# Attention and two mixers on one core: first weight blocks of the second mixer on another queue, token rows and operand steps in another order

## The chip, the cores and the metric

The kernel runs on one core of a Trainium2 chip. The metric is device time in microseconds (us). A run is one execution; the number given for a kernel is the median of its runs. One further execution was taken with the hardware profiler, and all rows come from that one.

## The reference

Three stages follow each other, for 2 batches of 768 tokens:

- clustered attention, 8 heads of 64: queries and keys get the best of 16 centroids; scores between different clusters are masked; softmax; product with `v`;
- a first mixer on the 512 channels: `u = x + (xT U V)T`, then `u + relu(u w_ch1) w_ch2` with 2048 hidden channels;
- a second mixer: `u = x + (relu(xT w_tok1) w_tok2)T` over tokens with 256 hidden rows, then `u + relu(u w_ch1) w_ch2` with 1536 hidden channels.

The change touches the passage from the channel part of the first mixer to the second mixer, and the channel part of the second mixer.

## The kernel before

Every large product is made of three matmuls on TensorE: a value is split into a rounded part ("hi") and the rest ("lo"), and hi x hi, hi x lo and lo x hi are added in PSUM. ScalarE rounds (`rnd(act, ...)`, L80), VectorE or GpSimd subtracts for the rest (`sub`, L87). A pair of these is called a cut: `cut(i, x, eng)` (L1030) returns the two steps, the second on `eng`.

**First mixer, channel part.** The order is a generator, `half_slots` (L888): 96 half-slots (`END`, L983), each either `hidden(k)` or `outmm(k)` of one of 48 units of 128 hidden channels, 12 matmuls of 512 columns each. The third pass (units 32 to 47) streams its weights from a scratch tensor in DRAM, `scr_a`: `feed` (L792) issues one load of 512 KB on ScalarE's DMA queue after most half-slots, into three slots used in turn. The counter `done` is the number of half-slots emitted. The last three are `hidden(47)` (done = 93), `outmm(46)` (94) and `outmm(47)` (95); after the last, four VectorE adds (L838) complete batch 1 of the residual `x2`.

**Beside it.** SyncE's queue (SP) stores the prepared second-mixer weights to `scr_b`: each `quad` (L616) converts a block and stores it in three transfers, 256, 512 and 1024 KB (L650 to L652). From half-slot 66 on, the token part of batch 0, `tok(0)` (L904), and the steps of `build_u(0)` (L1024) run beside the half-slots. `build_u(b)` makes the seven left operands of a seven-product (Strassen-like) scheme for the second mixer's channel part, `ops_u[b]`, from the four quarters `B` of `x2[b]`: three cuts of sums and quarters in a queue `todo` of 18 steps, popped one or two per half-slot; the last four (the cuts of operands 3 and 4) are left for the loop after the half-slots.

**Passage.** At done = 93, `turn_over` (L1048) opens the buffers of the second mixer and `load1(0)` to `load1(4)` are issued on SP's queue: `load1(n)` (L1069) fetches the n-th block of first-layer weights into one of five buffers `w1b` (four in a tile called `ring`, one in `wx`). Blocks 0, 1, 2 and 4 have 512 KB, block 3 has 256 KB. Later blocks are issued by `h_mm` on SP's queue as a buffer comes free. The program gives all transfers of both queues eight completion counters in turn, so a transfer can be issued only when the one eight before it has landed.

Then a loop of 14 steps (L1220) does the first-layer products of the first two pairs: `h_mm` (L1092), six matmuls of 384 columns into one PSUM bank, and `h_out` (L1108), which combines the seven products on ScalarE and VectorE. Beside them run the last four steps of `todo` (i = 1 and 2) and `tok(1)`, two of its steps at i = 1 to 8. The first six steps of `tok(1)` are its token rows: four transposes of `x2[1]` into PSUM bank 6 or 7 in turn, a copy on ScalarE (L916), a subtraction on VectorE (L917) that frees the bank.

**Second mixer, channel part.** Six runs `(b, k)` (L1236), three per batch, 14 steps each. A step does `h_mm` and `h_out` of the run after (`nxt`) and `o_mm` and `o_out` of this run. `o_out` (L1183) is a VectorE add of a PSUM bank into `x2`. `o_mm` of step i writes a bank that `o_out` of an earlier step must have read: four steps earlier inside a run, but two steps earlier at a run's start (the last products, steps 12 and 13, use the same banks as the first of the next run). During the runs 0 and 1 the 18 steps of `build_u(1)` are popped after `o_out`: one each at steps 5 to 13 of run 0, two each at steps 8 to 12 of run 1. Run 2 is the first to use them, in its `h_mm`. In `h_out`, s = 5 and s = 6 (steps 5, 7, 12 and 13) end with VectorE steps that only later products need.

All instructions of an engine run in the order written; a DMA issue stands in its engine's order too.

Of the kernel before, what the change touches and what calls it, by code (L numbers as in the profile page):

```python
# [16 lines left out]
ALU = mybir.AluOpType  # L17
# [9 lines left out]
def tile_cluster_attention__then__two_mixers(  # L27
# [996 lines left out]
    def build_u(b):  # L1024

        B = {(i, j): x2[b][:, 2 * i : 2 * i + 2, ts(j, HS)] for i in range(2) for j in range(2)}
        o = {i: ops_u[b][pos(i)] for i in ORDER}
        t = [fz[:, 768 * i : 768 * i + 768].rearrange("p (c n) -> p c n", c=2) for i in range(2)]

        def cut(i, x, eng):  # L1030
            hi, lo = o[i][:, 0], o[i][:, 1]
            return [lambda: rnd(act, hi, x), lambda: sub(eng, lo, x, f32(hi))]

        def add(o, x, y, op):
            return [lambda: dve.tensor_tensor(out=o, in0=x, in1=y, op=op)]  # L1035

        early, last = cut(4, t[1], dve), []
        if b == 0:
            early, last = last, early
        return (cut(1, B[0, 0], pool) + cut(2, B[1, 0], pool) + add(t[0], B[0, 0], B[0, 1], ALU.subtract)  # L1040
                + add(t[1], B[1, 1], t[0], ALU.add) + cut(6, t[1], dve) + add(t[1], B[1, 0], t[1], ALU.subtract) + early
                + cut(5, t[0], dve) + add(t[0], B[1, 1], B[0, 1], ALU.subtract) + cut(7, t[0], pool) + cut(3, B[1, 1], pool) + last)

    gfree = [x.rearrange("p (h n) -> p h n", h=2) for x in (qk_[:, ts(i, 2 * HS)] for i in range(14))]
    gs, behind = {}, []
# [20 lines left out]
    seq2 = [(b, k, c) for b, k in runs for c in range(4)]  # L1066
    at1, at2 = {}, {}

    def load1(n):  # L1069
        if n < len(seq1):  # L1070
            b, pr, c = seq1[n]
            ch = HCHUNKS[c]
            m, s0 = len(ch), min(STORED.index(i) for i in ch)
            x = w1b[n % len(w1b)][:, 0 : 512 * m]
            sp.dma_start(f32(x), scr2[pr, 0, :, 512 * s0 : 512 * (s0 + m)])
            for i in ch:
                at1[b, pr, i] = x[:, ts(STORED.index(i) - s0, 512)].rearrange("p (h n) -> p h n", h=2), n, i == ch[-1]

# [29 lines left out]
    def h_out(b, pr, s):  # L1108
# [28 lines left out]
        elif s == 2:  # L1137
            held_[0] = tmp()
            act.copy(held_[0], x)
        elif s == 3:  # L1140
            held_[3] = tmp()
            act.copy(held_[3], x)
        elif s == 4:
            new(3)
            dve.tensor_tensor(out=held_[3], in0=x, in1=held_[3], op=ALU.add)
            act.activation(held_[3], held_[3], AF.Relu)
            rnd(act, hi(3), held_[3])
            sub(dve, lo(3), held_[3], f32(hi(3)))
        elif s == 5:
            new(5, 6)  # L1150
            held_[5], held_[6] = tmp(), tmp()
            dve.tensor_tensor(out=held_[0], in0=x, in1=held_[0], op=ALU.add)
            relu_less(held_[5], held_[0], held_[1], ALU.subtract)
            rnd(act, hi(5), held_[5])
            sub(dve, held_[6], held_[3], held_[5])
            sub(dve, lo(5), held_[5], f32(hi(5)))
            cut(6, held_[6])
        else:
            new(2, 4, 7)
            top(2, x)  # L1160
            low(2, x)
            relu_less(held_[1], x, held_[6], ALU.subtract)
            relu_less(held_[5], held_[0], held_[3], ALU.subtract)
            behind.extend([lambda h=held_[5], c=cut: c(7, h), lambda h=held_[1], c=cut: c(4, h)])

    def o_mm(b, k, s, j):
        w, n, ends = at2[b, k, ORDER[s]]
# [35 lines left out]
    while done < END:  # L1203
        next(bg[1], None)
        next(t, None)
        if done == END - 3:
            for x in bg:
                for _ in x:
                    pass
            turn_over()  # L1210
            for n in range(len(w1b)):
                load1(n)
        k = done - first_tok
        for _ in range(int(16 <= k < 20) + 2 * int(k >= 20)):
            if len(todo) > 4:
                todo.pop(0)()
        advance(done + 1)

    t = tok(1)
    for i in range(14):  # L1220
        pr, s = divmod(i, 7)
        h_mm(0, pr, s)
        h_out(0, pr, s)
        for _ in range(2 * (0 < i < 3)):
            todo.pop(0)()
        for _ in range(1 + (1 <= i < 9) if i else 0):
            next(t, None)
        if i == 9:
            load2(0)
# [2 lines left out]
        pass  # L1232
    for n in range(2, len(w2b)):
        load2(n)
    todo = []
    for r, (b, k) in enumerate(runs):  # L1236
        nxt = runs[r + 1] if r + 1 < len(runs) else None
        if (b, k) == (0, 0):
            todo = build_u(1)
        for i in range(14):  # L1240
            if nxt:
                pr, s = divmod(i, 7)
# [1 line left out]
                h_mm(nxt[0], pr, s)  # L1244
            s_, j = divmod(i, 2)
            o_mm(b, k, s_, j)
            if nxt:
                for x in {6: (), 7: (6, 7)}.get(i, (i,)):
                    h_out(nxt[0], 2 * nxt[1] + x // 7, x % 7)
            if not nxt:  # L1250
                flush()
            o_out(b, k, s_, j)
            send(2 if nxt else 0)
            for _ in range(int(r == 0 and 4 < i) + 2 * int(r == 1 and i > 7)):
                if todo and (r == 1 or len(todo) > 9):
                    todo.pop(0)()
    send(0)


# [39 lines left out]
```

## Time and profile before

| what | value |
|---|---|
| runs | 742.27, 741.26, 742.25 us; median 742.25 us |
| profiled execution | 742.89 us, of which its span (first to last instruction) is 741.1 us |
| TensorE busy | 724.3 us, 98% of the span |
| VectorE, ScalarE, GpSimd busy | 72%, 55%, 27% |
| moved by DMA | 165.36 MB, mean 223 GB/s |
| chain that ended last | 84% TensorE, 8% VectorE, 3% DMA, 3% ScalarE |

TensorE is nearly always busy, so what the kernel can lose or win without other arithmetic lies in the short stretches in which TensorE stands. In a timeline row the two numbers ahead are the start and the length in us; `x12` is the number of instructions merged into the row; the bracket at the end is the idle time of the engine before the row and what ended it. `PE` is TensorE, `DVE` VectorE, `ACT` ScalarE, `POOL` GpSimd; `ACTq` and `SPq` are the DMA issues of ScalarE's and SyncE's queues. Rounding and subtraction have one line each for the whole program (L80 and L87), so they are told apart by what they write. In the passage `u`, `wx`, `qk`, `vz` are places of operands of `build_u(0)`, `ug` those of the token rows, `mid` and `fz` temporaries, `xn` the residual.

### The profile page before, as it was taken

Reading aid. Unit: us, or ns where it says so; the run is one execution under the profiler, and the core shown is the slowest. Engines: PE = TensorE matmul, PEld = TensorE weight load, DVE = VectorE, ACT = ScalarE, POOL = GpSimd, SP = SyncE. Lnnn points to the kernel's source line nnn. Section 1 sums busy time; section 2 is a strip of 40 time slices with the busy share of each in tenths; the row PEclk is TensorE's granted clock in tenths of the full one; section 3 lists DMA queues with packets and bytes.
Section 4 is the critical chain, followed back from the end, with each engine's and each line's share of the span. In section 5 each row is a group of like instructions: output and inputs, shape, how many; then the busy total and the mean of one; then the engine's idle time right before and its main releaser. Section 6 shows DMA issues by size and latency. Waiting matters only on the chain.

```text
span 741.1 us, 11133 instructions
## 1 busy us (share of the span) xinstructions
PE 724.3 (98%) x4046; PEld 601.7 (81%) x4046; DVE 534.0 (72%) x814; ACT 404.4 (55%) x699; POOL 201.7 (27%) x169
## 2 busy tenths in 40 slices
PE   8999999999999999999999999999999989999997
PEld 6666766776777788888888888888779989899997
DVE  7868988877886458769679586698365677765564
ACT  6678778867788455454555363543253435344330
POOL 6232252322211122423222312223012412221121
PEclk9999999999999999999999999999999999999999
DMA  6898588785303353967684989799726877697745
GB/s 175 197 196 225 147 206 206 222 217 124 76 14 119 117 212 120 376 227 284 236 319 172 331 324 374 251 364 386 287 91 217 302 250 236 200 300 270 264 128 164
DMA packets 55862, 165.36 MB, mean 223 GB/s; under 512 B 7648, under 2 KB 16736, under 8 KB 52224
## 3 DMA queue, kind: packets, MB, share of 16 engines
q1 hardware_dynamic: 50768, 147.05, 61.6%
q10 hardware_dynamic: 5040, 17.60, 6.3%
q8 instruction: 32, 0.52, 0.3%
q14 instruction: 22, 0.18, 0.1%
HBM read 103.61 MB, written 41.94 MB: 196 GB/s over the span
## 4 chain that ended last, share of the span: by engine, by line
PE 84%; DVE 8%; DMA 3%; ACT 3%; issue 1%; POOL 0%; SPq 0%; DVEq 0%; ACTq 0%; POOLq 0%
PE ps L75 74%; PE ps L350 8%; DVE qk L87 1%; DMA qk<-scr_a 1%; DMA qk<-pt 1%; DVE xn L1187 1%; ACT qk L80 1%; DVE fz L1035 1%; DVE mid L1090 1%; PE ps L413 1%; DMA sq__82<-in_qT_dram 1%; PE ps L370 1%; PE ps L915 1%; DVE nm L328 1%; ACT p L333 0%
## 5 line engine op out<-in xcount | busy, mean ns | idle before, releaser
L75 PE MATMUL ps<-ug,qk 128*128 128x512 f32 x576 | 138.2, 391 | 1.0 <-DMA qk<-scr_a 1.0
L75 PEld LDWEIGHTS ps<-ug,qk 128*128 128x128 f32 x576 | 107.5, 188 | 23.3 <-ACT ug L820 1.4
L75 PE MATMUL ps<-qk 112*128 112x384 f32 (+2 forms) x480 | 114.7, 366 | 2.5 <-ACT p L333 1.8
L328 DVE TENSOR_REDUCE nm<-ps 128x1 f32<-128x768 f32 x96 | 91.2, 954 | 27.9 <-PE ps L75 27.2
L75 PE MATMUL ps<-qk,tt 128*128 128x384 f32 (+1 forms) x528 | 106.7, 341 | 4.4 <-DVE xn L1187 4.4
L75 PEld LDWEIGHTS ps<-qk,tt 128*128 128x128 f32 x528 | 94.0, 188 | 7.3 <-DVE xn L1187 6.3
L333 ACT ACTIVATE p<-ps,nm 128x768 f32<-128x768 f32 x96 | 86.3, 901 | 21.1 <-DVE nm L328 19.0
L350 PEld LDWEIGHTS ps<-ident,p 128*128 128x128 f32 x576 | 68.3, 140 | 32.9 <-issue 26.9
L350 PE MATMUL ps<-ident,p 128*128 128x128 f32 x576 | 91.2, 277 | 0.4 <-DVE pt L355 0.3
L75 PEld LDWEIGHTS ps<-qk 112*128 112x128 f32 (+1 forms) x480 | 80.6, 189 | 11.6 <-ACT p L333 5.5
L821 DVE SCALAR_TENSOR_TENSOR ug<-ps,ug 128x512 fp32r<-128x512 f32 x48 | 33.0, 688 | 62.5 <-ACT ug L820 62.5
L820 ACT ACTIVATE ug<-ps 128x512 fp32r<-128x512 f32 x48 | 28.7, 598 | 82.0 <-PE ps L75 81.9
L75 PE MATMUL ps<-pt,vr 128*64 128x384 f32 x384 | 72.1, 498 | 0.0
L357 ACT COPY pt<-ps 128x512 f32<-128x512 f32 x96 | 55.8, 587 | 26.6 <-PE ps L350 23.1
L87 POOL TENSOR_TENSOR qk<-c__78,qk 128x512 fp32r<-128x512 f32 (+1 forms) x24 | 33.5, 1420 | 110.0 <-ACT qk L80 89.0
L1187 DVE TENSOR_TENSOR xn<-ps,xn 128x384 f32<-128x384 f32 x84 | 45.4, 551 | 21.3 <-PE ps L75 21.3
L87 POOL TENSOR_TENSOR qk<-mid,qk 128x384 fp32r<-128x384 f32 x26 | 26.3, 1020 | 90.9 <-ACT qk L80 76.9
L75 PEld LDWEIGHTS ps<-pt,vr 128*64 128x64 f32 x384 | 23.5, 136 | 25.8 <-issue 25.6
L80 ACT ACTIVATE qk<-mid 128x384 fp32r<-128x384 f32 x53 | 27.2, 523 | 31.2 <-DVE mid L1090 29.9
L75 PE MATMUL ps<-ug,wx 128*128 128x512 f32 (+1 forms) x180 | 41.9, 379 | 0.0
L123 ACT ACTIVATE c__78<-c__77 128x1024 f32<-128x1024 f32 (+2 forms) x27 | 29.7, 1099 | 22.3 <-DMA c__77<-in_wa_dram 10.6
L87 POOL TENSOR_TENSOR am<-am,amx 128x384 f32<-128x384 f32 (+1 forms) x13 | 11.0, 843 | 109.4 <-DVE amx L241 74.9
(230 smaller groups left out, 1239.8 us busy)
## 6 DMA issues: line engine op xcount, KB each, us to landing
tt<-scr_b SPq DMA_DIRECT2D x18, 1024.0 KB, 5.9
c__77<-in_wa_dram SPq DMA_DIRECT2D x16, 1024.0 KB, 6.2
qk<-scr_a ACTq DMA_DIRECT2D x32, 512.0 KB, 7.1
ring<-scr_b SPq DMA_DIRECT2D x29, 512.0 KB, 4.8
c__77<-in_wb_dram SPq DMA_DIRECT2D x12, 1024.0 KB, 7.3
scr_a<-qk SPq DMA_DIRECT2D x16, 512.0 KB, 5.9
scr_b<-qk SPq DMA_DIRECT2D x8, 1024.0 KB, 10.4
scr_a<-wx SPq DMA_DIRECT2D x12, 512.0 KB, 6.1
```

What stands on the lines that cost most here:

```text
L75: pe.matmul(o, lhsT=l, rhs=r, start=start, stop=stop, **kw)
L80: act.activation(o, i, AF.Copy, scale=scale)
L87: eng.tensor_tensor(out=o, in0=a, in1=b, op=ALU.subtract)
L123: act.activation(dst, hi.bitcast(F32), AF.Abs, scale=2.0 ** -112)
L328: dve.tensor_reduce(out=nm[:, n % 4 : n % 4 + 1], in_=ps[:, b0 : b0 + 2, 0:HS], axis=AX.XY, op=ALU.max, negate=True)
L333: act.activation(p32[n % NP32].rearrange("p (j k) -> p j k", j=2), ps[:, b0 : b0 + 2, 0:HS], AF.Exp, bias=nm[:, n % 4 : n % 4 + 1], accum_ ...
L350: pe.transpose(ps[:, tb[j], ts(i, P)], p32[n % NP32][:, ts(c, P)], ident)
L357: act.copy(o, ps[:, tb[j], :])
L370: pe.transpose(ps[:, bk, ts(t, P)], osb[q % 2][:, ts(t, P)], ident)
L820: act.activation(gh, o, AF.Relu)
L821: dve.scalar_tensor_tensor(out=gl, in0=o, scalar=0.0, in1=f32(gh), op0=ALU.max, op1=ALU.subtract)
L1187: dve.tensor_tensor(out=o, in0=ps[:, OB2[j][CHAIN[s]], 0:HS], in1=o, op=ALU.add)
```

## The change

- `load1` takes an engine. Blocks 0 and 1 are issued on ScalarE's queue at done = 93, blocks 2 and 3 at done = 94, block 4 after the last half-slot; none of the five by SP.
- The first two token rows of batch 1 are emitted at done = 95, ahead of `outmm(47)`. The 14-step loop then takes two steps of `tok(1)` at i = 2 to 8, as before, and none at i = 1.
- `build_u(0)`: the cut of operand 4 stands before that of operand 3; its two steps are popped at done = 93 and 94, those of operand 3 before the loop.
- `build_u(1)`: the rests of operands 7 and 3 are made on VectorE, not GpSimd, and the 18 steps are popped by a table: 8 in run 0 (steps 0, 2, 3, 9, 10), 6 in run 1 (steps 0, 2, 8, 9, 10), 4 in run 2 (steps 0, 2, 3).
- `h_out` hands back its last steps for s = 5 and s = 6 as a function, and in the runs that is called after `o_out` of the step.

```diff
@@ -1034,12 +1034,11 @@
         def add(o, x, y, op):
             return [lambda: dve.tensor_tensor(out=o, in0=x, in1=y, op=op)]
 
-        early, last = cut(4, t[1], dve), []
-        if b == 0:
-            early, last = last, early
+        c4, c5, c7, c3 = cut(4, t[1], dve), cut(5, t[0], dve), cut(7, t[0], (pool, dve)[b]), cut(3, B[1, 1], (pool, dve)[b])
+        d5 = add(t[0], B[1, 1], B[0, 1], ALU.subtract)
         return (cut(1, B[0, 0], pool) + cut(2, B[1, 0], pool) + add(t[0], B[0, 0], B[0, 1], ALU.subtract)
-                + add(t[1], B[1, 1], t[0], ALU.add) + cut(6, t[1], dve) + add(t[1], B[1, 0], t[1], ALU.subtract) + early
-                + cut(5, t[0], dve) + add(t[0], B[1, 1], B[0, 1], ALU.subtract) + cut(7, t[0], pool) + cut(3, B[1, 1], pool) + last)
+                + add(t[1], B[1, 1], t[0], ALU.add) + cut(6, t[1], dve) + add(t[1], B[1, 0], t[1], ALU.subtract)
+                + (c5 + d5 + c7 + c4 + c3 if b == 0 else c4 + c5 + d5 + [c7[0], c7[1], c3[0], c3[1]]))
 
     gfree = [x.rearrange("p (h n) -> p h n", h=2) for x in (qk_[:, ts(i, 2 * HS)] for i in range(14))]
     gs, behind = {}, []
@@ -1066,13 +1065,13 @@
     seq2 = [(b, k, c) for b, k in runs for c in range(4)]
     at1, at2 = {}, {}
 
-    def load1(n):
+    def load1(n, eng=sp):
         if n < len(seq1):
             b, pr, c = seq1[n]
             ch = HCHUNKS[c]
             m, s0 = len(ch), min(STORED.index(i) for i in ch)
             x = w1b[n % len(w1b)][:, 0 : 512 * m]
-            sp.dma_start(f32(x), scr2[pr, 0, :, 512 * s0 : 512 * (s0 + m)])
+            eng.dma_start(f32(x), scr2[pr, 0, :, 512 * s0 : 512 * (s0 + m)])
             for i in ch:
                 at1[b, pr, i] = x[:, ts(STORED.index(i) - s0, 512)].rearrange("p (h n) -> p h n", h=2), n, i == ch[-1]
 
@@ -1152,16 +1151,25 @@
             dve.tensor_tensor(out=held_[0], in0=x, in1=held_[0], op=ALU.add)
             relu_less(held_[5], held_[0], held_[1], ALU.subtract)
             rnd(act, hi(5), held_[5])
-            sub(dve, held_[6], held_[3], held_[5])
-            sub(dve, lo(5), held_[5], f32(hi(5)))
-            cut(6, held_[6])
+
+            def rest(h5=held_[5], h6=held_[6]):
+                sub(dve, h6, held_[3], h5)
+                sub(dve, lo(5), h5, f32(hi(5)))
+                cut(6, h6)
+
+            return [rest]
         else:
             new(2, 4, 7)
             top(2, x)
             low(2, x)
             relu_less(held_[1], x, held_[6], ALU.subtract)
-            relu_less(held_[5], held_[0], held_[3], ALU.subtract)
+
+            def rest(h5=held_[5], h0=held_[0], h3=held_[3]):
+                relu_less(h5, h0, h3, ALU.subtract)
+
             behind.extend([lambda h=held_[5], c=cut: c(7, h), lambda h=held_[1], c=cut: c(4, h)])
+            return [rest]
+        return []
 
     def o_mm(b, k, s, j):
         w, n, ends = at2[b, k, ORDER[s]]
@@ -1208,22 +1216,31 @@
                 for _ in x:
                     pass
             turn_over()
-            for n in range(len(w1b)):
-                load1(n)
+            for n in range(2):
+                load1(n, act)
+        elif done == END - 2:
+            for n in range(2, 4):
+                load1(n, act)
+        elif done == END - 1:
+            t = tok(1)
+            for _ in range(2):
+                next(t)
         k = done - first_tok
-        for _ in range(int(16 <= k < 20) + 2 * int(k >= 20)):
-            if len(todo) > 4:
+        keep = 4 if done < END - 3 else 2
+        for _ in range(int(k >= 16) + int(20 <= k < END - 3 - first_tok)):
+            if len(todo) > keep:
                 todo.pop(0)()
         advance(done + 1)
 
-    t = tok(1)
+    load1(4, act)
+    for f in todo:
+        f()
     for i in range(14):
         pr, s = divmod(i, 7)
         h_mm(0, pr, s)
-        h_out(0, pr, s)
-        for _ in range(2 * (0 < i < 3)):
-            todo.pop(0)()
-        for _ in range(1 + (1 <= i < 9) if i else 0):
+        for f in h_out(0, pr, s):
+            f()
+        for _ in range(2 * int(2 <= i < 9) + int(i >= 9)):
             next(t, None)
         if i == 9:
             load2(0)
@@ -1232,11 +1249,11 @@
         pass
     for n in range(2, len(w2b)):
         load2(n)
-    todo = []
+    todo = build_u(1)
+    spread = {(0, 0): 2, (0, 2): 2, (0, 3): 1, (0, 9): 2, (0, 10): 1, (1, 0): 1, (1, 2): 2, (1, 8): 1, (1, 9): 1, (1, 10): 1,
+              (2, 0): 1, (2, 2): 2, (2, 3): 1}
     for r, (b, k) in enumerate(runs):
         nxt = runs[r + 1] if r + 1 < len(runs) else None
-        if (b, k) == (0, 0):
-            todo = build_u(1)
         for i in range(14):
             if nxt:
                 pr, s = divmod(i, 7)
@@ -1244,16 +1261,20 @@
                 h_mm(nxt[0], pr, s)
             s_, j = divmod(i, 2)
             o_mm(b, k, s_, j)
+            rest = []
             if nxt:
                 for x in {6: (), 7: (6, 7)}.get(i, (i,)):
-                    h_out(nxt[0], 2 * nxt[1] + x // 7, x % 7)
+                    for f in rest:
+                        f()
+                    rest = h_out(nxt[0], 2 * nxt[1] + x // 7, x % 7)
             if not nxt:
                 flush()
             o_out(b, k, s_, j)
+            for f in rest:
+                f()
             send(2 if nxt else 0)
-            for _ in range(int(r == 0 and 4 < i) + 2 * int(r == 1 and i > 7)):
-                if todo and (r == 1 or len(todo) > 9):
-                    todo.pop(0)()
+            for _ in range(spread.get((r, i), 0)):
+                todo.pop(0)()
     send(0)
 
 
```

## Rows read from the trace of the kernel before

**Rows 1.** Waits of TensorE, 240 to 741 us: total us, times, longest.

```profile
PE ps L75 <- DVE xn L1187: 4.4, 6, 1.0
PE ps L915 <- DVE ug L87: 2.0, 2, 1.8
PE ps L75 <- DMA qk<-scr_a: 1.0, 1, 1.0
```

**Rows 2.** Timeline of TensorE, 495 to 550 us: the passage.

```profile
527.38 5.74 PE L75 MATMUL ps<-ug,qk 128*128 128x512 f32 x24 [1.04 <-DMA qk<-scr_a]
532.96 2.25 PE L75 MATMUL ps<-u,ring 128*128 128x384 f32 x12
535.05 1.03 PE L915 MATMUL ps<-ident,xn 128*128 128x128 f32 x8
535.84 1.30 PE L75 MATMUL ps<-u,ring 128*128 128x384 f32 x6
...
543.61 2.93 PE L75 MATMUL ps<-ug,tt 128*128 128x512 f32 x12
```

**Rows 3.** Timeline of ScalarE and its DMA queue, 505 to 560 us.

```profile
519.26 0.85 ACT L80 ACTIVATE wx<-fz 128x768 fp32r<-128x768 f32 x1 [3.10 <-DVE fz L1035]
519.32 0.33 ACTq L800 DMA_DIRECT2D qk<-scr_a  x1
...
521.08 0.33 ACTq L800 DMA_DIRECT2D qk<-scr_a  x1
526.38 0.60 ACT L820 ACTIVATE ug<-ps 128x512 fp32r<-128x512 f32 x1 [4.78 <-PE ps L75]
...
537.63 1.05 ACT L916 CAST ug<-ps 128x512 fp32r<-128x512 f32 x2
```

**Rows 4.** Timeline of SP's DMA queue, 440 to 560 us.

```profile
517.40 0.32 SPq L652 DMA_DIRECT2D scr_b<-qk  x1
517.81 6.01 SPq L1075 DMA_DIRECT2D ring<-scr_b  x4
```

**Rows 5.** Waits of SP's DMA queue, 516 to 530 us.

```profile
SPq L1075 <- DMA scr_b<-qk: 4.5, 2, 2.8
```

**Rows 6.** DMA queues, 520 to 525 us; q1 is SP's, q10 ScalarE's.

```profile
DMA packets 416, 2.07 MB, mean 414 GB/s; under 512 B 40, under 2 KB 40, under 8 KB 289
...
q1 hardware_dynamic: 328, 1.70, 83.4%
q10 hardware_dynamic: 87, 0.35, 16.9%
```

**Rows 7.** Timeline of VectorE, 518 to 570 us.

```profile
538.23 1.29 DVE L87 TENSOR_TENSOR ug<-ps,ug 128x512 fp32r<-128x512 f32 x2 [0.65 <-ACT ug L916]
539.84 0.96 DVE L87 TENSOR_TENSOR vz<-fz,vz 128x768 fp32r<-128x768 f32 x1 [0.33 <-ACT vz L80]
```

**Rows 8.** VectorE timeline, 569 to 637 us: end of run 1.

```profile
633.69 1.95 DVE L1090 SCALAR_TENSOR_TENSOR mid<-fz,mid 128x384 f32<-128x384 f32 x1
```

**Rows 9.** Timeline of GpSimd, 560 to 741 us: the same moment.

```profile
633.38 1.84 POOL L87 TENSOR_TENSOR u<-xn,u 128x768 fp32r<-128x768 f32 x1
```

**Rows 10.** VectorE timeline, 637 to 741 us: ends of runs 2 and 4.

```profile
664.42 1.01 DVE L1187 TENSOR_TENSOR xn<-ps,xn 128x384 f32<-128x384 f32 x2
...
721.87 0.56 DVE L1090 SCALAR_TENSOR_TENSOR qk<-ps,qk 128x384 fp32r<-128x384 f32 x1
...
723.27 1.01 DVE L1187 TENSOR_TENSOR xn<-ps,xn 128x384 f32<-128x384 f32 x2
```

**Rows 11.** TensorE timeline, 609 to 741 us: starts of runs 3, 5.

```profile
665.69 1.23 PE L75 MATMUL ps<-qk,tt 128*128 128x384 f32 x6
...
721.98 1.33 PE L75 MATMUL ps<-qk,tt 128*128 128x384 f32 x6 [0.43 <-DVE xn L1187]
723.87 13.79 PE L75 MATMUL ps<-qk,tt 128*128 128x384 f32 x78 [0.56 <-DVE xn L1187]
```

**Rows 12.** Timeline of ScalarE, 715 to 726 us: end of run 4.

```profile
721.36 0.47 ACT L1118 ACTIVATE qk<-ps 128x384 fp32r<-128x384 f32 x1
```

## The prediction

> **What bounds the kernel now.** I first read the waits of TensorE in the second half of the span [rows 1]: it stood for an output's sum six times, 4.4 us, for a token row twice, 2.0 us, and for streamed weights once, 1.0 us. Between these it works without a break, so the change can win only what these waits and the small pauses beside them cost, and lose only by making new ones.
>
> Then the timeline of the passage [rows 2]. TensorE stops at 527.38 - 1.04 = 526.34 and reaches the first batch of token products at 543.61: 17.27 us. The work inside is 24 matmuls of the last two half-slots (532.96 - 527.38 = 5.58), five steps of `h_mm` (twelve matmuls take 535.05 - 532.96 = 2.09, so 1.045 a step, 5.23) and 24 transposes (eight take 535.84 - 535.05 = 0.79, so 2.37): 13.18 us. So 17.27 - 13.18 = 4.09 us of the passage are not work; 1.04 + 2.0 of them are named in [rows 1], 1.0 are pauses between shorter waits.
>
> Why it stood: the load that `outmm(46)` needs was issued only at 519.32, since ScalarE, which issues it, first stood 3.10 us for a sum of `build_u(0)` [rows 3]. SP had put a 1 MB store at 517.40 and ring blocks from 517.81 on in its own queue [rows 4]. From 520 to 525 us the engines moved 414 GB/s, 83.4% of the busy share for SP's queue and 16.9% for ScalarE's [rows 6]. The token rows were late because their copies stand on ScalarE behind the roundings of operand 3 and the `h_out` steps (537.63), and their subtractions at 538.23 and later, with operand 4's rest among them [rows 3, 7].
>
> At the run starts TensorE waits for `o_out` of steps 12 and 13 of the run before. Of the six waits two are at the start of run 5 (0.43 and 0.56) [rows 11]; the other 4.4 - 0.99 = 3.4 us are four more rows of this form, two each at the starts of runs 1 and 2, which follow the runs with steps of `build_u(1)`. Runs 3 and 4 start without one: the sum of step 13 of run 2 starts at 664.42 and is over by about 665.0, its bank is wanted at 665.69 [rows 10, 11]. One reason stands in [rows 8, 9]: a VectorE step on SBUF operands that takes 0.56 elsewhere [rows 10] took 1.95, while GpSimd made a rest for 1.84; `o_out` was behind it.
>
> **The change, part by part.**
>
> *Loads on ScalarE's queue.* Five issues of 0.33 us each [rows 3] now stand in ScalarE's order: two fall into its idle 4.78 us before 526.38, two behind that instruction and one behind the copies of the token rows, where it has nothing due for 2 us; they cost nothing on the path. SP's queue loses them and holds nothing else that is late. Blocks 0 and 1 now start behind the load of 521.08, some 3.7 us later than at 517.81. From 521.5 they have 11 us until `h_mm` starts, at about 532.7 by the walk below. Nothing before the issue of 519.32 changes; the same steps of `todo` are popped until then. The gain is the 1.0 MB of blocks 0 and 1 that no longer runs beside that load: at 414 GB/s [rows 6] 2.5 us of the engines' time, of which at least 1.04 must have gone ahead of it to be worth the wait. Bounds: 0 (all of it went behind) and 1.04 (no more is lost there). I take 1.04, as SP's queue had five times the share of ScalarE's.
>
> The Trainium skill speaks against this part ("Trainium Kernel Development and Optimization", Key Constraints): transfers issued by SyncE, ScalarE and GpSimd run on the same 16 DMA engines and interleave, and a second issuer saves only issue time. By that the loads would still share the engines with the weights, and this term would be 0. The shares in [rows 6], far from equal, show that the order of issue mattered here; whether a later start is enough, no row shows.
>
> *Token rows.* The first two are made between `outmm(46)` and `outmm(47)`: eight transposes, 0.79 us, only moved; their two copies (1.05) and subtractions (1.29) [rows 3, 7] lie beside the 2.79 us of `outmm(47)`. Banks 6 and 7 are then free when rows 3 and 4 come. What is late next: rows 5 and 6 wait for rows 3 and 4. Walk: 526.34 + 2.79 (`outmm(46)`) + 0.79 + 2.79 = 532.7; three steps of `h_mm` to 535.85; eight transposes to 536.65; step 3 to 537.7. On ScalarE the copies of rows 3 and 4 stand behind step 1's two roundings, which follow a VectorE add, and step 2's copy; they start about 536.9 and take 1.05, the subtractions (0.6 each) free the banks at about 538.25 and 538.85. TensorE stands 538.25 - 537.7 = 0.55 there and 0.2 to 0.3 for the other bank, 0.85 in sum. So of 4.09 us 0.85 stays and **3.2 us** go, the 1.04 of the loads among them. Bounds: 0.5 (only the moved rows help, and most of that is lost to the next bank) and 4.1.
>
> *Operands 4 and 3 of batch 0.* ScalarE rounds operand 4 in its idle time before 526.38 [rows 3]; VectorE's 0.96 [rows 7] moves out of the token rows to before the last adds. Operand 3 is rounded before the loop and its rest made on GpSimd by about 534, its first use is step 5. Cost nothing; the gain is in the walk above.
>
> *Steps of `build_u(1)`.* Same number, 18. VectorE gets two more (the rests of 7 and 3, 0.96 each, 1.9 us), GpSimd two fewer. In run 0 GpSimd's two rests move to steps 0 and 2, where a VectorE step may stand up to 1.84 [rows 9] behind them; the next sum is wanted four steps, 8.4 us, later, so this is hidden. At steps 9 and 10 of runs 0 and 1 two VectorE steps of 0.96 remain and none after; they fill its idle time but for about 0.4 us, against 0.7 us to spare at the end of run 2 [rows 10, 11]. In run 2 operands 7 and 3 are finished one step, about 2.1 us, before `h_mm` wants them: a sum, then 0.96, leaves about 0.4. So **3.4 us** go. Bounds: 1.6 (the waits at step 13 stay) and 3.4.
>
> *A sum ahead.* At the end of run 4 step 12's sum passes two VectorE steps, so its wait of 0.43 goes. For step 13 only one step of three is passed, and ScalarE's relu (721.36 [rows 12]), which stands behind the rounding of the held-back steps, comes about 0.35 later; the two steps left then start at 722.2 in place of 721.87 and the sum at 723.13 in place of 723.27 [rows 10]. What counts is when TensorE goes on for good at 723.87 [rows 11]: **0.14 us** earlier. Bounds: 0 and 0.99.
>
> **The sum.** 3.2 + 3.4 + 0.14 = 6.8 us. Against the profiled execution, 742.89, this gives 736.1; that execution is 0.64 longer than the median of the runs, 742.25, so the forecast for the median is 742.25 - 6.8 = **735.5 us**. Its own range, with small misses of the walk: 734.6 to 736.4.
>
> **The rivals.**
> 1. *The weights stay late.* The load of 519.32 still competes with SP's 1 MB store and the rest of its 512 KB one, and lands after 526.34 as before. For: its issue is not earlier. Against: a megabyte beside it is gone. The 1.04 us stay: 736.5 us. It is also what the sentence of the Trainium skill cited above ("Trainium Kernel Development and Optimization", Key Constraints) would make of this part.
> 2. *VectorE still lags at the run starts.* If the two steps at 9 and 10 cost 0.7 us instead of 0.4, or a rest on GpSimd stretches one, the second wait at the starts of runs 1 and 2 stays, about 0.9 each: 735.5 + 1.8 = 737.3 us. For: 0.7 us to spare is one VectorE step. Against: GpSimd makes none of the new steps there.
> 3. *Slower: ScalarE stands in front of a load.* SP waited 4.5 us in two waits before ring loads, up to 2.8, for older stores to land [rows 5]. Now ScalarE would wait, and behind it stand the activation of unit 47, the token copies and `h_out`. The second pair of loads is issued at about 527.0; the copy of step 0 is due at 533.8. Each us past that moves the rest by one; slower than before from 533.8 + 6.8 = 540.6 on, a wait of 13.6 us. With a wait of 15 us: 743.7. Against: the last such store was issued at 517.40 [rows 4], 9.6 us before that pair.
> 4. *No difference.* The waits only change their names, in the passage and at the run starts alike: 742.
>
> **How the numbers follow.** Forecast 0.55; rival 1 0.17; rival 2 0.16; both of them (738.3) 0.04; rival 3 0.04; rival 4 0.04. The range takes in the forecast and rivals 1 and 2, alone and together: 734.3 to 738.3. A change of 0.2%, 1.5 us, is about what a measurement of this kernel can tell from none. Faster by more than that are the forecast and rivals 1 and 2: 0.92; the same 0.04; slower 0.04.
>
> **What would show it.** In the trace after: no wait for `scr_a` before the 24 matmuls, or one of about 1 us (rival 1); `L915` waits of about 0.5 to 0.9 us in all; no wait for `xn L1187` at the starts of runs 1 and 2; one of about 0.8 us left at run 5. ScalarE's ring issues should show no wait over a microsecond. The passage from the end of `hidden(47)` to the first token product should take about 14 us. I am wrong if a wait on a ring block stands before `h_mm`, or on operands 7 or 3 of batch 1 in run 2.

## The result, and the profile after

The changed kernel takes 734.07 us (median of 4 runs, 733.49 to 734.66); the kernel before took 741.75 us beside it (4 runs, 740.47 to 742.27). The ratio is 0.9896, 95% interval 0.9881 to 0.9911: 7.7 us faster, where 6.8 were forecast. The forecast of 735.5 us had the direction and, for the weights and the run starts, the mechanism, but the time lies 0.2 us below the range.

The page of the changed kernel: span, busy times, and the chain that ended last by engine.

```profile
span 732.6 us, 11123 instructions
...
PE 721.4 (98%) x4046; PEld 601.7 (82%) x4046; DVE 532.2 (73%) x816; ACT 404.2 (55%) x699; POOL 198.2 (27%) x167
...
PE 92%; DVE 3%; DMA 2%; ACT 1%; issue 1%; POOL 0%; SPq 0%; DVEq 0%; ACTq 0%; POOLq 0%
```

The chain is now 92% TensorE, where it was 84%, and VectorE's share fell from 8% to 3%. The waits of TensorE in the second half of the span, with the columns of [rows 1] (the changed kernel's `o_out` adds in L1195):

```profile
PE ps L75 <- DVE xn L1195: 1.2, 1, 1.2
PE ps L915 <- DVE ug L87: 0.5, 1, 0.5
```

Of the nine waits of [rows 1] two are left: one for a token row, one for a sum. Where the time came from is best read from start to start of things that both kernels do. Three marks serve: the start of ScalarE's activation of unit 47 (526.38 in [rows 3]), the first token product (543.61 in [rows 2]), and the start of the last sum of the kernel, a `xn` add of VectorE (737.71 before, 729.19 after).

| stretch | before, us | after, us | less |
|---|---|---|---|
| activation of unit 47 to first token product | 17.23 | 14.24 | 2.99 |
| first token product to last sum | 194.10 | 189.47 | 4.63 |
| both | 211.33 | 203.71 | 7.62 |

This is the 7.7 us of the medians. (The first mark itself came 0.90 us sooner in the profiled execution after, which is the run of 734.41 us, in a part that the change hardly touches. Over all kernels below it falls between 524.1 and 526.4 us, so whole times scatter more than these stretches.)

**The passage**, TensorE's timeline, which answers to [rows 2]:

```profile
500.76 27.64 PE L75 MATMUL ps<-ug,qk 128*128 128x512 f32 x120
528.24 1.03 PE L915 MATMUL ps<-ident,xn 128*128 128x128 f32 x8
529.02 3.02 PE L75 MATMUL ps<-ug,qk 128*128 128x512 f32 x12
531.88 3.29 PE L75 MATMUL ps<-u,ring 128*128 128x384 f32 x18
535.01 1.03 PE L915 MATMUL ps<-ident,xn 128*128 128x128 f32 x8
...
537.57 1.25 PE L915 MATMUL ps<-ident,xn 128*128 128x128 f32 x8 [0.47 <-DVE ug L87]
...
539.72 2.93 PE L75 MATMUL ps<-ug,tt 128*128 128x512 f32 x12
```

The 24 matmuls of the last two half-slots show no wait any more (a pause of 0.2 us that no bracket shows is left there, see e7); the transposes of the first two token rows stand between them (528.24). One wait of 0.47 us is left, at rows 5 and 6. ScalarE and its queue, which answers to [rows 3]:

```profile
518.36 0.85 ACT L80 ACTIVATE wx<-fz 128x768 fp32r<-128x768 f32 x1 [3.10 <-DVE fz L1035]
518.42 0.33 ACTq L800 DMA_DIRECT2D qk<-scr_a  x1
...
520.12 0.33 ACTq L800 DMA_DIRECT2D qk<-scr_a  x1
520.54 1.36 ACTq L1074 DMA_DIRECT2D ring<-scr_b  x2
...
525.48 0.60 ACT L820 ACTIVATE ug<-ps 128x512 fp32r<-128x512 f32 x1 [2.68 <-PE ps L75]
```

The rounding at 518.36 still waits 3.10 us, and the load behind it is still issued only then (518.42). The ring blocks follow at 520.54. The shares of the two queues from 520 to 525 us, which answers to [rows 6]:

```profile
q10 hardware_dynamic: 294, 1.10, 54.8%
q1 hardware_dynamic: 143, 0.94, 45.2%
```

ScalarE's queue now has the larger share. The load of 518.42 landed 6.8 us after its issue, at 525.2; the one of 519.32 before took 7.9.

**The run starts.** TensorE's timeline of the kernel before at the start of run 1, then that of the changed kernel:

```profile
599.17 1.20 PE L75 MATMUL ps<-u,ring 128*128 128x384 f32 x6
601.37 1.33 PE L75 MATMUL ps<-qk,tt 128*128 128x384 f32 x6 [1.00 <-DVE xn L1187]
602.54 1.21 PE L75 MATMUL ps<-u,ring 128*128 128x384 f32 x6
604.67 1.31 PE L75 MATMUL ps<-qk,tt 128*128 128x384 f32 x6 [0.93 <-DVE xn L1187]
605.82 1.21 PE L75 MATMUL ps<-u,ring 128*128 128x384 f32 x6
```

```profile
595.28 1.21 PE L75 MATMUL ps<-u,ring 128*128 128x384 f32 x6
596.33 1.23 PE L75 MATMUL ps<-qk,tt 128*128 128x384 f32 x6
...
599.50 1.21 PE L75 MATMUL ps<-u,ring 128*128 128x384 f32 x6
```

In the kernel before the four groups from 599.17 take 605.82 - 599.17 = 6.65 us; the same four after take 599.50 - 595.28 = 4.22. So 2.43 us went, though the two bracketed waits add up to 1.93 only. At run 2 it is the same: 631.08 to 637.31 before, 6.23 us; 624.76 to 628.92 after, 4.16; 2.07 us, where the brackets say 1.50. VectorE at the end of run 0 in the changed kernel, the sums of steps 12 and 13:

```profile
594.33 0.55 DVE L1195 TENSOR_TENSOR xn<-ps,xn 128x384 f32<-128x384 f32 x1
...
597.31 0.55 DVE L1195 TENSOR_TENSOR xn<-ps,xn 128x384 f32<-128x384 f32 x1
```

They are over by about 594.9 and 597.9; their banks are wanted at 596.33 and 598.43.

**Run 5.** TensorE (the start of step 13's `o_mm`, and of the last 78 matmuls) and VectorE behind it (the relu of step 13, its sum):

```profile
711.93 2.27 PE L75 MATMUL ps<-qk,tt 128*128 128x384 f32 x12
715.36 13.79 PE L75 MATMUL ps<-qk,tt 128*128 128x384 f32 x78 [1.15 <-DVE xn L1195]
```

```profile
713.81 0.56 DVE L1089 SCALAR_TENSOR_TENSOR qk<-ps,qk 128x384 fp32r<-128x384 f32 x1 [0.56 <-ACT qk L1117]
...
714.75 0.55 DVE L1195 TENSOR_TENSOR xn<-ps,xn 128x384 f32<-128x384 f32 x1
```

TensorE's one wait of 1.15 took the place of two; from step 13's `o_mm` to the last stretch it is 715.36 - 711.93 = 3.43 us, before 723.87 - 720.33 = 3.54.

### The profile page after: what moved, and what is told of

Same layout as the page of the kernel before. It is cut to its first block, busy times and chain, and to the rows that moved or that the text cites. A ratio compares the mean times of both kernels' runs of the same rounds, so it can differ in the third digit from the quotient of the medians.

```text
span 732.6 us, 11123 instructions
## 1 busy us (share of the span) xinstructions
PE 721.4 (98%) x4046; PEld 601.7 (82%) x4046; DVE 532.2 (73%) x816; ACT 404.2 (55%) x699; POOL 198.2 (27%) x167
## 4 chain that ended last, share of the span: by engine, by line
PE 92%; DVE 3%; DMA 2%; ACT 1%; issue 1%; POOL 0%; SPq 0%; DVEq 0%; ACTq 0%; POOLq 0%
PE ps L75 82%; PE ps L350 8%; DMA qk<-pt 1%; PE ps L413 1%; PE ps L370 1%; PE ps L915 1%; DMA sk__83<-in_kT_dram 0%; ACT p L333 0%; DMA cc<-in_cen_dram 0%; DVE xn L1195 0%; DVE nm L328 0%; POOL qk L87 0%; ACT pt L80 0%; ACT qk L80 0%; DVE am L250 0%
## 5 line engine op out<-in xcount | busy, mean ns | idle before, releaser
L1195 DVE TENSOR_TENSOR xn<-ps,xn 128x384 f32<-128x384 f32 x84 | 46.1, 553 | 17.9 <-PE ps L75 17.6
```

Of the source, the lines that this page charges most:

```text
L1195: dve.tensor_tensor(out=o, in0=ps[:, OB2[j][CHAIN[s]], 0:HS], in1=o, op=ALU.add)
```

## The experiments

Each is the changed kernel with an edit, unless said otherwise. All stretches below are from the same three marks, in the trace of each.

| kernel | unit 47 to token product, us | token product to last sum, us | ratio to before, 95% interval |
|---|---|---|---|
| before | 17.23 | 194.10 | 1 |
| changed | 14.24 | 189.47 | 0.9896 (0.9881 to 0.9911) |
| e1 loads on SP | 15.45 | 189.44 | 0.9898 (0.9879 to 0.9917) |
| e2 old steps | 15.01 | 191.51 | 0.9915 (0.9894 to 0.9936) |
| e3 no sum ahead | 14.20 | 189.60 | 0.9868 (0.9848 to 0.9888) |
| e4 rows late | 15.46 | 189.52 | 0.9903 (0.9885 to 0.9922) |
| e5 operands late | 17.24 | 190.53 | 0.9933 (0.9920 to 0.9945) |
| e6 last run's banks | 14.57 | 188.05 | 0.9874 (0.9860 to 0.9887) |
| e7 load unblocked, SP | 14.01 | 189.46 | 0.9879 (0.9866 to 0.9893) |
| e8 banks, unblocked | 14.16 | 188.06 | 0.9853 (0.9839 to 0.9866) |
| e9 operands alone | 16.55 | 189.50 | 0.9895 (0.9864 to 0.9925) |
| e10 all, row banks | 13.16 | 188.04 | 0.9837 (0.9812 to 0.9863) |
| e11 old places, VectorE | 14.45 | 194.24 | 0.9949 (0.9930 to 0.9968) |
| e12 new places, GpSimd | 14.40 | 189.63 | 0.9888 (0.9856 to 0.9919) |

The kernel before was timed anew beside each set, at medians from 741.75 to 743.42 us, so ratios are compared, not times (they are not the quotients of the medians); differences of a microsecond lie inside their intervals, and there the traces decide. e3 shows how far that goes: its ratio is lower than the changed kernel's, though its two stretches together are 0.09 us longer; its first mark came 1.4 us sooner, in a part that both share.

**e1, the loads back on SP's queue.**

```diff
-            for n in range(2):
-                load1(n, act)
-        elif done == END - 2:
-            for n in range(2, 4):
-                load1(n, act)
+            for n in range(len(w1b)):
+                load1(n)
...
-    load1(4, act)
```

> The changed kernel, with the five ring blocks issued on SP's queue at done = 93 again. Theory (they ran beside the load that outmm(46) needs): that load lands 7.9 us after its issue in place of 6.8, a wait of about 1.0 us stands before outmm(46) again, the kernel takes 735.1 in place of 734.1. Rival (the loads share the engines from either queue, so the queue does not matter): no wait there and no difference in time.

```profile
527.57 2.99 PE L75 MATMUL ps<-ug,qk 128*128 128x512 f32 x12 [1.18 <-DMA qk<-scr_a]
```

The wait is back at 1.18 us, and the passage takes 1.21 longer. In this form the place of the loads is worth what the theory said.

**e7, the same with the load issued sooner.** To e1's edit comes this: operand 7's two steps go one half-slot later.

```diff
-            if len(todo) > keep:
+            if k != 24 and len(todo) > keep:
```

> The changed kernel with the ring blocks on SP's queue again (as in e1) and operand 7's two steps popped one half-slot later, so that ScalarE does not stand 3.1 us in front of the load that outmm(46) needs. Theory (the late issue is the cause, and the ring blocks only made a tight landing miss): the load is issued near 515 in place of 518.4 and there is no wait for it, 14.2 us from unit 47's activation to the first token product. Rival (the traffic on SP's queue is the cause): the wait of about 1.2 us stays, 15.4.

ScalarE's queue (two loads from 514.62 on; in the changed kernel the second went out at 518.42), and SP's ring blocks:

```profile
514.62 0.85 ACTq L800 DMA_DIRECT2D qk<-scr_a  x2
```

```profile
516.84 6.76 SPq L1074 DMA_DIRECT2D ring<-scr_b  x4
```

No wait, 14.01 us, with the ring blocks on SP's queue as early as before. The second load was issued 3.4 us sooner than in the changed kernel (515.04 against 518.42), and landed by 524.6, 9.6 us after its issue; TensorE was free for it at 525.4. So with SP's traffic beside it, what made the load late was its place in ScalarE's order, behind a rounding that waits for VectorE; the traffic used up the little time that this left. The changed kernel treats the second cause and keeps the first: three of its variants with the same loads had a wait of 0.18 (e11), 0.33 (e6) and 0.41 us (e4) there, and e2 one of 0.72 (its load was issued at 518.51 and landed 7.6 us later, at 526.1; TensorE went on at 526.26).

The changed kernel itself was not quite in time either. From the mark to the first transposes it takes 528.24 - 525.48 = 2.76 us, e7 527.94 - 525.41 = 2.53: the 0.23 us by which the passages differ. TensorE's loading of weights (`PEld`), which runs ahead of the matmuls, stood there in the changed kernel for the completion counter of this load (landed at 525.2), and not in e7:

```profile
525.36 2.61 PEld L75 LDWEIGHTS ps<-ug,qk 128*128 128x128 f32 x12 [0.35 <-issue]
```

Counted in this way the pause at the load was 1.3 us in the kernel before, 0.2 in the changed kernel and 1.4 in e1.

**e4, the token rows late.**

```diff
-        elif done == END - 1:
-            t = tok(1)
-            for _ in range(2):
-                next(t)
...
+    t = tok(1)
...
-        for _ in range(2 * int(2 <= i < 9) + int(i >= 9)):
+        for _ in range(2 * int(1 <= i < 9) + int(i >= 9)):
```

> The changed kernel, with the first two token rows of batch 1 at step 1 of the loop again; operands 3 and 4 stay ahead of the loop. Theory (rows 3 and 4 wait for the banks of rows 1 and 2): a wait of 1 to 1.8 us before the third row's transposes, 1 to 2 us more, 735.1 to 736.1. Rival (what cost time there was ScalarE's rounding of operand 3 in the loop, which is gone): under 0.5 us more.

```profile
525.69 5.74 PE L75 MATMUL ps<-ug,qk 128*128 128x512 f32 x24 [0.41 <-DMA qk<-scr_a]
...
536.58 1.25 PE L915 MATMUL ps<-ident,xn 128*128 128x128 f32 x8 [1.14 <-DVE ug L87]
```

The wait that the theory named is there, 1.14 us, and the one of 0.47 at the next two rows is gone. The passage is 1.22 us longer, but the pause at the load, which has nothing to do with the edit, is 0.6 here (0.41 and 0.2 that the bracket leaves out) and 0.2 in the changed kernel. That leaves 0.8 for the rows: between the theory's 1 and the rival's 0.5.

**e5, the operands late.**

```diff
-        keep = 4 if done < END - 3 else 2
+        keep = 4
...
-    for f in todo:
-        f()
...
+        for _ in range(2 * (0 < i < 3)):
+            todo.pop(0)()
```

The order of the two cuts goes back too, operand 3 ahead of operand 4.

> The changed kernel, with the cuts of operands 3 and 4 of batch 0 in the loop again (steps 1 and 2, 3 ahead of 4). The late token rows alone cost 0.65 us of the passage's 3.0 and the loads 1.2, so 1.1 are left for this part. Theory (ScalarE's two roundings of 0.85 and VectorE's rest of 0.95 stand ahead of the copies and subtractions of rows 3 and 4): 1.1 us more from unit 47's activation to the first token product, 15.3 in place of 14.24. Rival (the parts overlap, each hides the other): under 0.4 us more.

TensorE's third pair of transposes and the first token product; ScalarE ahead of them (the two roundings of operands 3 and 4, then the copies of rows 3 and 4); and VectorE, on which operand 4's rest stands ahead of the subtractions of rows 3 and 4, which free the banks:

```profile
539.87 1.25 PE L915 MATMUL ps<-ident,xn 128*128 128x128 f32 x8 [2.99 <-DVE ug L87]
...
542.50 4.00 PE L75 MATMUL ps<-ug,tt 128*128 128x512 f32 x12
```

```profile
535.62 0.83 ACT L80 ACTIVATE qk<-xn 128x768 fp32r<-128x768 f32 x1
...
536.72 0.84 ACT L80 ACTIVATE vz<-fz 128x768 fp32r<-128x768 f32 x1
537.46 1.06 ACT L916 CAST ug<-ps 128x512 fp32r<-128x512 f32 x2
```

```profile
537.59 1.62 DVE L87 TENSOR_TENSOR vz<-fz,vz 128x768 fp32r<-128x768 f32 x1 [1.28 <-ACT vz L80]
539.13 1.28 DVE L87 TENSOR_TENSOR ug<-ps,ug 128x512 fp32r<-128x512 f32 x2
```

This one part undone takes back the whole gain of the passage, 17.24 us, and 1.1 more behind it (190.53 - 189.47), though the loads and the first rows stay where the change put them. Neither theory said so much. TensorE stands 2.99 us in one piece, 2.5 more than in the changed kernel, and the rest is its clock: the group behind those transposes lasts 1.62 us to the next start where it lasted 1.14 (539.72 - 538.58), and the token product 546.34 - 542.50 = 3.84 where 2.77 is usual. The table by stretch of e5, with the granted clock in the third column from the end:

```profile
538.00:542.00 4.00, 2.13 (x13) 1.96 (x14) 3.23 (x5) 2.07 (x5) 0.39 (x1) 0.92 0.41 124
542.00:546.00 4.00, 4.00 (x14) 3.30 (x13) 1.58 (x3) 1.04 (x2) 0.00 (x0) 0.65 0.02 4
546.00:550.00 4.00, 4.00 (x21) 3.44 (x20) 2.23 (x4) 1.16 (x3) 0.04 (x1) 1.00 0.23 66
```

From full speed (2.4 GHz) the mean fell to 0.92 and 0.65 of it after that wait, so part of the time went at 1.2 GHz, and it was 1.00 again behind. This cost 0.48 + 1.07 = 1.6 us. After the 1.84 us of the kernel before, one step of the loop sooner, the clock stayed at 1.00 and the token product took its usual 2.77 (543.61 to 546.38).

**e9, the operands alone** (the edits of e1 and e4 together).

> The changed kernel with the ring blocks on SP's queue (as in e1) and the token rows late (as in e4): of the passage's three parts only the earlier operands 3 and 4 are left. From unit 47's activation to the first token product the changed kernel takes 14.24, the kernel before 17.23. Theory (the three parts act on one chain, VectorE's and ScalarE's, of which the operands are the longest piece): 15.5 to 16.1, since e1 and e4 lost 1.2 and 0.65 to 1.2. Rival (the parts only work together): 17 and more.

16.55 us, between both. The wait for weights was 1.51 there, a pause of 1.7 us from start to start where the changed kernel has 0.2; the rest of the difference to the changed kernel, 2.31 - 1.5 = 0.8, is the rows, as in e4. The operands alone are worth 17.23 - 16.55 = 0.7, or 1.2 when the wait for weights, 0.47 longer here than in the kernel before, is left out. So of the 2.99 us some 1.0 are the loads (pauses of 1.3 and 0.2), 1.2 the operands and 0.8 the rows, in that order. But counted from the other end the loads and the rows are worth only 0.5 without the operands (17.23 - 17.24 + 0.48, e5 without its clock), less than the loads by themselves: early rows with late operands lost some 0.5. Rows and operands lie on one chain, ScalarE's copies and VectorE's subtractions, and the operands' roundings and operand 4's rest stand at its head.

**e2, e3, e11, e12: the run starts.** e2 puts the steps and the engine of `build_u(1)` back:

```diff
-        c4, c5, c7, c3 = cut(4, t[1], dve), cut(5, t[0], dve), cut(7, t[0], (pool, dve)[b]), cut(3, B[1, 1], (pool, dve)[b])
+        c4, c5, c7, c3 = cut(4, t[1], dve), cut(5, t[0], dve), cut(7, t[0], pool), cut(3, B[1, 1], pool)
...
-            for _ in range(spread.get((r, i), 0)):
-                todo.pop(0)()
+            for _ in range(int(r == 0 and 4 < i) + 2 * int(r == 1 and i > 7)):
+                if todo and (r == 1 or len(todo) > 9):
+                    todo.pop(0)()
```

> The changed kernel, with the 18 steps of build_u(1) popped where they were (steps 5 to 13 of run 0, 8 to 12 of run 1) and the rests of operands 7 and 3 on GpSimd; the sum stays ahead. Theory (these steps make VectorE late at the starts of runs 1 and 2, and that cost 4.5 us from start to start, not the 3.4 us of the waits' idle column): the waits come back, less up to two VectorE steps of 0.5 at each start that the sum ahead passes: 2.5 to 4.5 us more, 736.6 to 738.6. Rival (the sum ahead alone removes these waits): under 1 us more.

```profile
600.64 1.33 PE L75 MATMUL ps<-qk,tt 128*128 128x384 f32 x6 [0.84 <-DVE xn L1195]
...
630.63 1.32 PE L75 MATMUL ps<-qk,tt 128*128 128x384 f32 x6 [0.27 <-DVE xn L1195]
```

One wait at each start; in the stretch it is 191.51 - 189.47 = 2.04 us: under the theory's 2.5, over the rival's 1. e3 puts the last steps of `h_out` ahead of the sum again:

```diff
-                    rest = h_out(nxt[0], 2 * nxt[1] + x // 7, x % 7)
+                    for f in h_out(nxt[0], 2 * nxt[1] + x // 7, x % 7):
+                        f()
```

> The changed kernel, with the last steps of h_out for s = 5 and 6 back ahead of o_out. Theory (the sum ahead is worth 0.1 us at run 5 and nothing at runs 1 and 2, whose steps now leave room): 734.2, no wait at the starts of runs 1 and 2, two waits again at run 5. Rival (it is what clears the starts of runs 1 and 2): waits there again, 1 to 2 us more.

```profile
712.19 1.31 PE L75 MATMUL ps<-qk,tt 128*128 128x384 f32 x6 [0.43 <-DVE xn L1195]
714.08 13.80 PE L75 MATMUL ps<-qk,tt 128*128 128x384 f32 x78 [0.57 <-DVE xn L1195]
```

Only run 5 differs, by 0.13 us: with the steps at their new places the sum ahead is worth nothing at runs 1 and 2, and the new places alone win 194.10 - 189.60 = 4.50 us. With the steps at the old places the sum ahead wins 194.10 - 191.51 = 2.59, some 0.1 of it at run 5: in this stretch e2 differs from the kernel before by nothing else. So these two parts, too, are not to be added up. The last two split the new table, both with e3's edit. e11 has besides the second part of e2's edit (the old places, the rests on VectorE); e12 has the first (the new places, the rests on GpSimd).

> The changed kernel without the sum ahead (as in e3), with the 18 steps popped where they were, but the rests of operands 7 and 3 on VectorE. The kernel before lost 4.5 us from start to start at runs 1 and 2, 2.45 and 2.05. Theory (the place of the steps counts, not the engine): 3 to 4.5 us more than e3 from the first token product to the last run. Rival (GpSimd's rests, which hold VectorE, are the cause): run 2's start is clear, run 1's is not, 2 to 2.5 us more.

```profile
597.01 1.33 PE L75 MATMUL ps<-qk,tt 128*128 128x384 f32 x6 [0.96 <-DVE xn L1195]
...
600.30 1.32 PE L75 MATMUL ps<-qk,tt 128*128 128x384 f32 x6 [0.92 <-DVE xn L1195]
...
628.66 1.33 PE L75 MATMUL ps<-qk,tt 128*128 128x384 f32 x6 [0.75 <-DVE xn L1195]
...
631.94 1.32 PE L75 MATMUL ps<-qk,tt 128*128 128x384 f32 x6 [0.90 <-DVE xn L1195]
```

Old places, rests on VectorE: 194.24 - 189.60 = 4.64 us more than e3, all four waits are back. The brackets add up to 3.53; the cost is 1.1 more, the same surplus as in the kernel before. In this stretch e11 differs from the kernel before by the engine of the two rests alone, 194.24 against 194.10: at the old places the engine counts for nothing.

> The changed kernel without the sum ahead (as in e3), the steps at their new places, but the rests of operands 7 and 3 on GpSimd, at steps 2 and 3 of run 2. Theory (they are finished one step before their use, and GpSimd takes 1.84 in place of 0.95): waits of 0.3 to 1 us before h_mm of steps 4 and 5 of run 2, 0.5 to 1.5 us more than e3. Rival (h_mm has slack enough): the same as e3 within 0.3 us.

New places, rests on GpSimd: 189.63, the same as e3. The rival was right: the engine counts for nothing at the new places either, and the places do all of it.

**e6, e8, e10: what is left.** The last run's products go to banks that `h_mm` has left:

```diff
+    ob = lambda b, k: ((4, 5), (1, 7)) if (b, k) == (NB - 1, NG - 1) else OB2
...
-        o, on = ps[:, OB2[j][CHAIN[s]], 0:HS],
+        o, on = ps[:, ob(b, k)[j][CHAIN[s]], 0:HS],
...
-        dve.tensor_tensor(out=o, in0=ps[:, OB2[j][CHAIN[s]], 0:HS], in1=o, op=ALU.add)
+        dve.tensor_tensor(out=o, in0=ps[:, ob(b, k)[j][CHAIN[s]], 0:HS], in1=o, op=ALU.add)
```

> The changed kernel, with the last run's products in four PSUM banks that h_mm has left (4, 5, 1 and 7 in place of 2, 3, 6 and 7). Theory (what is left at run 5's start is the wait for the banks of steps 12 and 13): no wait there, 1.3 us less from start to start, 732.8 where the changed kernel takes 734.1. Rival (VectorE is late there as such, and its adds then hold the tail): the last matmuls start sooner, the end moves by under 0.4 us.

```profile
712.24 15.79 PE L75 MATMUL ps<-qk,tt 128*128 128x384 f32 x90
```

The last 90 matmuls run in one piece; 1.42 us less from the token product to the last sum. e8 adds e7's edit, with the ring blocks on ScalarE's queue.

> The changed kernel with both: the last run's free banks and operand 7's steps one half-slot later, ring blocks on ScalarE's queue. Theory: the weights land 3 us before their use, so no execution meets a wait there, and run 5 starts without one: 732.7, at or under e6. Rival (the load issued sooner takes bandwidth from the one of unit 47's first half, and hidden(47) waits): 0.5 us or more over e6.

The gain at run 5 is there (188.06), and no bracket for weights; the passage takes 14.16 us. But the weights did not land 3 us before their use, as the theory said: issued at 514.04, the load took 10.1 us, landed at 524.1, and left a pause of 0.1 us. e10 adds free banks for the last two token rows:

```diff
-            k = nbk()
+            k = nbk() if b == 0 or s < 4 else s - 2
```

> e8 with the last two token rows of batch 1 transposed into banks 2 and 3, which stand free there, in place of 7 and 6. Theory (the wait of 0.47 and the pause behind it are for the banks of rows 3 and 4): no wait in the passage, 0.5 to 0.7 us less than e8, 13.5 us from unit 47's activation to the first token product. Rival (the copies and subtractions of rows 5 and 6 then hold the token products): the wait only moves to these, under 0.2 us less.

```profile
535.78 1.03 PE L915 MATMUL ps<-ident,xn 128*128 128x128 f32 x8
...
537.71 2.93 PE L75 MATMUL ps<-ug,tt 128*128 128x512 f32 x12
```

13.16 us, 1.0 less than e8 where 0.5 to 0.7 was expected, and no wait is left in the passage; this is the 13.18 us of pure work that the prediction counted. With 731.29 us (6 runs) against 742.48 beside it, e10 has the lowest ratio of all, 0.9837. Its interval overlaps that of e8 (0.9839 to 0.9866), and both lie clear of the changed kernel's.

## Why the prediction missed

- **The sum of the run starts was the step that failed:** "So **3.4 us** go. Bounds: 1.6 (the waits at step 13 stay) and 3.4." Every wait of runs 1 and 2 did go, but they had cost 2.43 + 2.07 = 4.50 us. The upper bound was the sum of the idle column, and that is no bound: in [rows 11] a group of six matmuls is given as 1.23 long, while the next normally starts 1.05 after it. The idle time in the bracket is counted from that end, so some 0.2 us of each wait is hidden in the row before it, and the group after a wait takes longer too (from 601.37 to 602.54 it is 1.17, not 1.05). Four waits were short by 1.07 us in all; e11 shows the same surplus, 4.64 against 3.53. With 4.5 in its place the sum would have been 7.8 and the forecast 734.4, the range lower by 1.1.
- **The rest of the miss is no step of the working.** Of the 1.4 us between forecast and time, 1.1 are the run starts; the passage takes 0.2 back; and 0.5 lie in the kernel before, which took 741.75 us beside the changed kernel and not the 742.25 from which the forecast was counted. From 742.25 the measured gain of 7.7 would have given 734.6, inside the range: that the time fell just outside is in part chance. (The sum's 6.8 comes of the terms before rounding, 3.24 and 3.41.)
- **The passage was right:** 3.2 forecast, 2.99 measured. It was worked out from start to start, less the work in between, and so did not have this fault. What stayed was 1.1 us in place of 0.85: 0.85 at the place named (14.01 in e7 less 13.16 in e10) and 0.2 at the load.
- **The loads:** the pause fell from 1.3 to 0.2 us, about the 1.04 forecast. But the reason given, traffic beside the load, was half of it: e7 has e1's traffic and no wait. Nor does e1 (1.21 us) speak against the sentence of the Trainium skill cited there ("Trainium Kernel Development and Optimization", Key Constraints), by which a second issuer saves only issue time: e1 changes queue and time of issue of the ring blocks together (516.8 on SP, 520.5 on ScalarE), and no run separates the two.
- **The token rows and operands:** the prediction gave the operands no price of their own ("Cost nothing; the gain is in the walk above") and put the gain on the rows. The runs show the larger part with the operands: the rows are worth 0.8, and that only with the operands early (e4, e5); the operands are worth 1.2 by themselves (e9) and 2.5 in waiting alone once the rows are early (e5). The walk was right because it contained both; the credit was not.
- **The steps of `build_u(1)`:** that places count was right (e11). The suspicion of GpSimd was not: its rests did hold a VectorE step ([rows 8, 9]), but with them at the new places nothing is lost (e12), and without them at the old places nothing is won (e11).
- **A sum ahead:** 0.14 us forecast, 0.11 measured by TensorE's starts, 0.13 by e3, and by the mechanism named: the relu comes later.
- Rival 2 did not happen in the changed kernel. Of rival 1 0.2 us remained, and five variants had more. Of rival 3 a little was seen, without harm: ScalarE's first two ring issues took 1.36 us where the next two took 0.81, so it stood some 0.5 us there, and 1.1 in e2 and e12 (1.94); operand 4's rounding stood behind them, but its rest on VectorE followed only at 526.72.

## What to carry to other kernels

Size a wait from start to start, against the same stretch where nothing waits, not by the idle time that stands in the row: with pipelined matmuls here the rows showed 3.43 of 4.50 us at the run starts, 0.47 of 0.85 at the token rows (e7 against e10), and nothing of 0.2 at the load. When several parts feed one chain, undoing each in turn does not share out the gain; ask which stands at the head. And of a load that is late ask also where its issue stands in its engine's order, before the traffic beside it alone is blamed.

## What was not expected of the hardware

The same load, issued at the same place of the program, landed 0.2 us too late in some executions and 1.0 in another, with the DMA engines at 402 to 411 GB/s. Counted from start to start against e7 the pause was 0.2 us in the changed kernel, e3 and e5 and 0.4 in e12 (none of which shows a bracket), 0.4 in e11, 0.6 in e6 and e4, 1.0 in e2. From issue to landing the load took 6.8 us in the changed kernel, 7.0 in e12, 7.2 in e6, 7.3 in e4, 7.6 in e2. Here a landing worked out to a few tenths of a microsecond was a chance, not a fact: issued 3.4 us sooner it took 9.5 to 10.1 us, so that it landed in time in e7 and e10 and 0.1 us late in e8, which runs the same code as e10 up to there.

The clock of TensorE fell after one wait of 2.99 us (e5), and not after one of 1.84 one step of the loop sooner (before); it turned a wait of 2.5 us more into a loss of 4.1. Where a wait is sized, what the engine does at a lower clock behind it belongs to its price. Each of the two stands on one trace.
